# Other column orders for reads and sums of the first layer in one set of blocks

## The chip, the cores and the metric

The kernel runs on one core of a Trainium2 chip. The metric is the device time of one execution in microseconds (us). The engines are named as the profile names them: PE is TensorE (PEld its weight loads), DVE is VectorE, ACT is ScalarE, POOL is GpSimd, SP is SyncE, which here only issues DMAs.

## What is computed

Each of 8 batches of 2496 rows of 256 values is convolved with a filter by FFTs along the rows. The 19968 results then go through a mixture of experts: a gate picks two of eight experts for each row, and each expert is two matrix products with a ReLU between them.

```
X = np.fft.rfft(x, axis=1)
y = np.fft.irfft(X * F, n=x.shape[1], axis=1)
...
logits = x @ w_gate
noise_scale = np.log1p(np.exp(x @ w_noise))
noisy_logits = logits + noise_scale * noise
top2 = np.argpartition(-noisy_logits, 2, axis=1)[:, :2]
...
for e in range(E):
    for k in range(2):
        mask = top2[:, k] == e
        h = np.maximum(x[mask] @ w1[e], 0.0)
        out[mask] += top2_w[mask, k, None] * (h @ w2[e])
```

The sizes are D = 256, F = 1024 hidden values and E = 8 experts.

## The kernel before

The FFT of a batch is written as matrix products with small tables (`s1`, `kg0` to `kg2`, `t3`, `i2`), then come the gate and the routing of the batch (`gate`, `route`). They put the row numbers that each expert has to do into lists in DRAM. As soon as a batch is routed, the experts can work on blocks of 512 listed rows while the FFT of the next batches goes on beside them. `run` deals the blocks out in sets: set 1 has 2 blocks, set 2 another 10, set 3 another 4. Set 4, which starts when the fourth batch is routed, has 4 pairs, so 8 blocks; later sets follow up to the eighth batch, then the rests. Each block carries the number of its set in `ready`.

A block goes through `expert` like this. Its 512 rows are gathered from DRAM by GpSimd (line 1005), turned by a DMA transpose, and split into a rounded part `mxh` and a remainder `mxl` (lines 1066 and 1067), for each of the two halves `kc` of the 256 input values. Then the first layer runs over eight column blocks `f` of 128 hidden values. For each, `_mm3` is called for the two `kc`: six products (lines 123 to 125) with weights `w1h` or `w1l` as the standing operand and the 512 rows of `mxh` or `mxl` as the moving one. All six add into one bank `hps` of 128 x 512 fp32 sums. Two banks bear the tag `hps`; in these blocks every third sum uses the single bank `xps`, so three banks take turns. ACT writes the ReLU of the sums, rounded, into `hh` (line 1156), DVE the remainder into `hl` (line 1157). That eviction frees the bank.

The second layer takes 128 rows at a time: from set 4 on (`WIDE`), line 1183 multiplies `hh` with both parts of `w2` side by side, and line 1184 multiplies `hl` with the rounded part, for eight `f`. ACT and DVE add the two halves of the bank `yps` (lines 1188 and 1190), and GpSimd adds the rows into the output by an indirect DMA (line 1191).

The products of the FFT that the prediction speaks of: line 353 transposes 128 x 128 blocks next to one another into a bank; line 430 writes four results of 128 columns into a bank with `q3[:, :, 2 * j:2 * j + 2].rearrange("p b r -> p r b")`, so neighbours in time lie eight fp32 apart. In `route`, line 928 multiplies fp16 tables; in the first two batches the four tables `j` lie interleaved in a tile, so that both operands are read at a step of four fp16 values (8 bytes), in later batches they lie one behind another. Line 526 copies fp32 results as two 2-byte halves, read at a step of 4 bytes.

The order of each engine's instructions isn't written by hand here: the framework schedules them with a simulated timeline in which each engine works in order. The pace of FFT work against expert work is set by `PACE` and `FILL`. Waits are semaphores that the framework adds where tiles or banks are shared.

Of the kernel before, what the change touches and what calls it, by code (L numbers as in the profile page):

```python
# [15 lines left out]
AF = mybir.ActivationFunctionType  # L16
ALU = mybir.AluOpType
# [104 lines left out]
def _mm3(nc, o, lh, ll, rh, rl, start=True, stop=True):  # L122
    nc.tensor.matmul(o, lh, rh, start=start, stop=False)  # L123
    nc.tensor.matmul(o, lh, rl, start=False, stop=False)  # L124
    nc.tensor.matmul(o, ll, rh, start=False, stop=stop)  # L125


def f32v(ap):
    return ap.bitcast(F32)
# [9 lines left out]
BANKS = {"hps": 2, "yps": 2, "xps": 1, "fps": 3}  # L139

MOVES = {0: {"q3": "yps"}, 12: {"q3": "fps"}, 14: {"q3": "yps", "q4": "yps", "q5": "hps", "q6": "hps"}, 26: {"q4": "fps", "q5": "yps", "q6": "yps"}}


class Moe:
# [390 lines left out]
    def fft_stream(self):  # L535
# [105 lines left out]
        for t in range(max(plan) + 1):  # L641
            self.banks.update(MOVES.get(t, {}))
            for g in plan.get(t, []):
# [481 lines left out]
    def expert(self, parts, may, fill=None):  # L1125

        nc, P = self.nc, self.P
        self.parts, self.ahead, self.standing, self.early_l = parts, [], False, None
        self.fetch(lambda: True)
        cur = None  # L1130
        while self.ahead:
            if cur is None:
                cur = self.front(self.ahead[0], fill)
            ent = self.ahead.pop(0)
            blk, i = ent[:2]
            lt, n, nt, s, tabi, ready = blk
            w = 128 * nt
            w1, xT, w2st = cur
            if i == 0:
                w2, adds = [], []  # L1140
            ids, gate = lt[:, i], xT[2]
            if not self.ahead or self.ahead[0][3] or sum(len(a[2][0]) for a in self.ahead) < 4:
                self.fetch(may)
            third = ("xps", 1) if self.by_dma(ent) else ("yps", 2)
            hh = []
            for f in range(8):

                tag, bufs = ("hps", 2) if f % 3 < 2 else third
                p = self.PS.tile([128, 512], F32, name="hps", tag=tag, bufs=bufs)[:, :w]
                for kc in range(2):  # L1150
                    wh, wl = w1[f // 2]
                    o = (f % 2) * 128
                    _mm3(nc, p, wh[:, kc, o:o + 128], wl[:, kc, o:o + 128], *xT[kc], start=(kc == 0), stop=(kc == 1))
                h = P.tile([128, 512], R32, name="hh", bufs=8)[:, :w]
                l = P.tile([128, 512], R32, name="hl", bufs=8)[:, :w]
                nc.scalar.activation(h, p, AF.Relu)  # L1156
                v = nc.vector.scalar_tensor_tensor(l, p, 0.0, f32v(h), op0=ALU.max, op1=ALU.subtract)  # L1157
                if f == 4:
                    self.early_l = v
                hh.append((h, l))  # L1160
                if f % 2 and i == 0:
                    w2.append(self.wsplit(w2st[f // 2], "w2", f // 2))
                yield
            late = not self.ahead
            if late:
                self.fetch(lambda: True)
            if self.ahead:
                e2 = self.ahead[0]
                cur = (w1, self.turn(e2), None) if e2[1] else self.front(e2, fill if late else None)
            self.fetch(may)  # L1170
            yield
            for t in range(nt):


                wide = ready >= WIDE
                if wide or t % 2 == 0:
                    bank = self.PS.tile([128, 2, D], F32, name="yps", bufs=2)
                p = bank[:, 0 if wide else t % 2]
                for f in range(8):
                    h, l = (a[:, t * 128:(t + 1) * 128] for a in hh[f])  # L1180
                    hl = w2[f // 2][:, :, f % 2]
                    if wide:
                        nc.tensor.matmul(bank, h, hl, start=(f == 0), stop=False)  # L1183
                        nc.tensor.matmul(p, l, hl[:, 0], start=False, stop=(f == 7))  # L1184
                    else:
                        _mm3(nc, p, h, l, hl[:, 0], hl[:, 1], start=(f == 0), stop=(f == 7))
                o = self.slot("yo")
                nc.scalar.activation(o, p, AF.Copy, scale=gate[:, t])  # L1188
                if wide:
                    nc.vector.scalar_tensor_tensor(o, bank[:, 1], gate[:, t], o, op0=ALU.mult, op1=ALU.add)  # L1190
                a = nc.gpsimd.indirect_dma_start(  # L1191
                    out=self.io["out"][:BLK + ready * ROWS], out_offset=bass.IndirectOffsetOnAxis(ap=ids[:, t:t + 1], axis=0),
                    in_=o, in_offset=None, compute_op=ALU.add)
                for q in adds:
                    self.tc.declare_no_dep(a.ins, q.ins, reason="distinct rows of one expert")
                adds.append(a)
                self.lasta = a
                yield
# [109 lines left out]
```

## Time and profile before

| what | value |
|---|---|
| time, median of 3 runs | 2274.14 us (2271.94 to 2280.01) |
| span of the profiled execution, first to last instruction | 2263.0 us (the profile has no time of the whole execution beside it) |
| mean granted clock of TensorE | 0.992 |
| HBM read, written | 225.63 MB, 105.25 MB |
| products of the first layer in blocks of 512 rows (lines 123 to 125) | 1136 for each line |
| products of the second layer from set 4 on (lines 1183, 1184) | 2016 for each line |

How to read it: the page gives busy times of each engine over the span of one profiled execution. A row of a group shows line, engine, operation, output and inputs, shapes and count, then busy time in all and the mean of one in ns, then idle time of the engine just ahead of them and what ended it. A row of the timeline begins with its start and its length in us; products follow one another in a pipeline, so the length of one reaches into the next, and the distance of two starts is its pace. A row of stretches gives from:to, its length, and the busy time of PE, PEld, DVE, ACT and POOL with instruction counts, then the granted clock, the DMA share and GB/s. A row of waits names the engine and line that waited, the one that ended the wait, the sum in us, how often, and the longest. Rows of one source line give min/median/max in ns and the first and last start.

### The profile page before, as it was taken

How to read it: one execution, taken by the hardware profiler on the slowest of the kernel's cores; microseconds unless marked ns; L12 is line 12 of the kernel's file. 1: busy time of each engine (PE TensorE's matmuls, PEld its weight loads, DVE VectorE, ACT ScalarE, POOL GpSimd, SP SyncE). 2: the span in 40 equal slices, each digit the busy share in tenths (PEclk: the TensorE clock that was granted, in tenths of full speed). 3: DMA queues.
4: the chain of work that ended last, by engine and by line, in shares of the span. 5: the costliest groups of instructions: out<-in, count | busy, mean ns of one | idle time of the engine just before them, and what ended most of it. 6: DMA issues, size and time to landing. Idle time of an engine off the chain costs nothing.

```text
span 2263.0 us, 39152 instructions
## 1 busy us (share of the span) xinstructions
PE 2201.1 (97%) x12535; PEld 1838.5 (81%) x12535; DVE 1621.3 (72%) x3494; ACT 1239.4 (55%) x2425; POOL 953.5 (42%) x821
## 2 busy tenths in 40 slices
PE   8779999999999999999999999999999999999998
PEld 5438888888778788888888888888888888889997
DVE  4858689779777977697668866695555555667886
ACT  6765655666565455545544455443444444557876
POOL 4013344334233543344434544355454544554442
PEclk9989999999999999999999999999999999999999
DMA  8678778887686676668665667555555556768774
GB/s 242 189 229 203 186 185 190 205 201 169 144 223 156 151 170 154 149 142 178 143 146 121 134 131 165 108 125 121 124 117 115 116 127 125 180 158 244 217 212 130
DMA packets 436441, 368.99 MB, mean 163 GB/s; under 512 B 187675, under 2 KB 347395, under 8 KB 436227
## 3 DMA queue, kind: packets, MB, share of 16 engines
q1 hardware_dynamic: 374915, 282.01, 45.7%
q0 software_dynamic: 61312, 84.40, 23.2%
q8 instruction: 100, 1.64, 0.3%
q14 instruction: 114, 0.93, 0.1%
HBM read 225.63 MB, written 105.25 MB: 146 GB/s over the span
## 4 chain that ended last, share of the span: by engine, by line
PE 88%; ACT 3%; DMA 3%; DVE 3%; issue 2%; SPq 1%; POOL 0%; ACTq 0%; POOLq 0%; DVEq 0%
PE yps L1183 20%; PE hps L123 13%; PE hps L124 12%; PE hps L125 12%; PE yps L1184 10%; PE yps L123 2%; PE yps L125 2%; PE yps L124 2%; PE q L430 2%; PE q L494 1%; PE u L441 1%; DMA stage<-y,ids 1%; PE q L319 1%; PE q L518 1%; PE q L519 1%
## 5 line engine op out<-in xcount | busy, mean ns | idle before, releaser
L1191 POOL DMA_INDIRECT out<-stage,ids x316 | 535.8, 1696 | 450.8 <-DVE stage L1190 222.2
L1183 PE MATMUL yps<-w,hh 128*128 128x512 f32 x2016 | 710.7, 398 | 1.6 <-DVE stage L1190 1.4
L1005 POOL DMA_INDIRECT stage<-y,ids x316 | 337.2, 1067 | 538.4 <-DMA xt<-stage 403.7
L1184 PE MATMUL yps<-w,hl 128*128 128x256 f32 x2016 | 539.1, 282 | 0.0
L124 PE MATMUL hps<-mxl,w1h 128*128 128x512 f32 (+2 forms) x1424 | 530.5, 374 | 0.3 <-DVE mxl L1067 0.3
L125 PE MATMUL hps<-mxh,w1l 128*128 128x512 f32 (+2 forms) x1424 | 524.4, 370 | 0.0
L123 PE MATMUL hps<-mxh,w1h 128*128 128x512 f32 (+2 forms) x1424 | 518.8, 376 | 2.0 <-DVE hl L1157 1.6
L1157 DVE SCALAR_TENSOR_TENSOR hl<-hps,hh 128x512 fp32r<-128x512 f32 (+2 forms) x712 | 433.2, 624 | 94.2 <-ACT hh L1156 91.8
L1156 ACT ACTIVATE hh<-hps 128x512 fp32r<-128x512 f32 (+2 forms) x712 | 380.5, 553 | 205.1 <-PE hps L125 186.4
L1183 PEld LDWEIGHTS yps<-w,hh 128*128 128x128 f32 x2016 | 368.3, 188 | 80.4 <-issue 1.9
L1184 PEld LDWEIGHTS yps<-w,hl 128*128 128x128 f32 x2016 | 378.9, 189 | 28.6 <-issue 1.7
L1188 ACT ACTIVATE stage<-yps,gt 128x256 f32<-128x256 f32 x316 | 142.6, 478 | 368.1 <-PE yps L1184 213.6
L125 PEld LDWEIGHTS hps<-mxh,w1l 128*128 128x128 f32 x1424 | 268.2, 188 | 48.8 <-issue 0.6
L124 PEld LDWEIGHTS hps<-mxl,w1h 128*128 128x128 f32 x1424 | 268.7, 189 | 41.3 <-DVE mxl L1067 0.7
L123 PEld LDWEIGHTS hps<-mxh,w1h 128*128 128x128 f32 x1424 | 264.3, 189 | 45.5 <-DVE hl L1157 6.5
L1190 DVE SCALAR_TENSOR_TENSOR stage<-yps,gt,stage 128x256 f32<-128x256 f32 x252 | 115.9, 479 | 221.7 <-ACT stage L1188 220.6
L1113 ACT CAST w1h<-stage 128x512 fp32r<-128x512 f32 x188 | 116.6, 621 | 107.0 <-PE hps L124 57.1
L1114 DVE TENSOR_TENSOR w1l<-stage,w1h 128x512 fp32r<-128x512 f32 x188 | 128.0, 685 | 55.2 <-ACT w1h L1113 54.3
L1114 DVE TENSOR_TENSOR w<-stage,w 128x512 fp32r<-128x512 f32 x224 | 149.7, 684 | 9.9 <-ACT w L1113 9.7
L123 PE MATMUL yps<-w,hh 128*128 128x256 f32 x512 | 145.7, 288 | 3.2 <-ACT hh L1156 2.8
L1113 ACT CAST w<-stage 128x512 fp32r<-128x512 f32 x224 | 137.7, 637 | 9.8 <-DMA stage<-w 5.5
L124 PE MATMUL yps<-w,hh 128*128 128x256 f32 x512 | 142.9, 285 | 0.0
(226 smaller groups left out, 3004.9 us busy)
## 6 DMA issues: line engine op xcount, KB each, us to landing
stage<-w SPq DMA_DIRECT2D x412, 256.0 KB
x<-x SPq DMA_DIRECT2D x88, 256.0 KB
fd<-c SPq DMA_DIRECT2D x77, 240.0 KB
wb<-w SPq DMA_DIRECT2D x18, 1024.0 KB
fx<-fd SPq DMA_DIRECT2D x140, 128.0 KB
out<-z SPq DMA_DIRECT2D x24, 702.0 KB
y<-yt SPq DMA_DIRECT2D x40, 248.6 KB
y<-yt SPq DMA_DIRECT2D x40, 234.0 KB
```

The source lines that it names most:

```text
L123: nc.tensor.matmul(o, lh, rh, start=start, stop=False)
L124: nc.tensor.matmul(o, lh, rl, start=False, stop=False)
L125: nc.tensor.matmul(o, ll, rh, start=False, stop=stop)
L1005: self.pin(lambda: nc.gpsimd.indirect_dma_start(out=x.bitcast(I32), out_offset=None, in_=self.y[:BLK + ready * ROWS], in_offset=bass.Indir ...
L1113: nc.scalar.copy(h, sv)
L1114: nc.vector.tensor_sub(l, sv, f32v(h))
L1156: nc.scalar.activation(h, p, AF.Relu)
L1157: v = nc.vector.scalar_tensor_tensor(l, p, 0.0, f32v(h), op0=ALU.max, op1=ALU.subtract)
L1183: nc.tensor.matmul(bank, h, hl, start=(f == 0), stop=False)
L1184: nc.tensor.matmul(p, l, hl[:, 0], start=False, stop=(f == 7))
L1188: nc.scalar.activation(o, p, AF.Copy, scale=gate[:, t])
L1191: a = nc.gpsimd.indirect_dma_start(out=self.io["out"][:BLK + ready * ROWS], out_offset=bass.IndirectOffsetOnAxis(ap=ids[:, t:t + 1], axis= ...
```

## The change

Only blocks with `ready == 4` are touched, in `expert`. A table `WALKS` gives for each column block `f` an order in which the six products read their 512 moving rows (`read`) and one in which they write the sums (`put`). `walk` makes the operand's access pattern: "odd" takes every other row first and then the rest, a number i takes i rows of the first half, i of the second half, the next i of the first, and so on.

| f | moving rows are read | sums are written | pieces of the eviction |
|---|---|---|---|
| 0, 7 | in order | in order | 1 |
| 1 | every other one | in order | 2 |
| 2 | runs of 2, by turns from both halves | the same order, so each sum is at its own place | 1 |
| 3 | in order | runs of 2, by turns into both halves | 2 |
| 4, 5, 6 | runs of 2, 4, 8, by turns from both halves | in order | 2 |

Where `read` and `put` differ, the sums lie in another order in the bank than the rows have; `pairs` then cuts the eviction into two pieces of 256 columns, each with patterns on bank and tile that put the values back into order. Each piece is one ACTIVATE on ACT and one SCALAR_TENSOR_TENSOR on DVE.

```diff
+WALKED = 4
+WALKS = [(None, None), ("odd", None), (2, 2), (None, 2), (2, None), (4, None), (8, None), (None, None)]
+def walk(a, how):
+    if how is None:
+        return a
+    if how == "odd":
+        return a.rearrange("p (j two) -> p two j", two=2)
+    return a.rearrange("p (h j i) -> p j h i", h=2, i=how)
+def halves(a, how):
+    if how is None:
+        return [a[:, 256 * h:256 * h + 256] for h in range(2)]
+    a = a.rearrange("p (j h) -> p h j", h=2) if how == "odd" else a.rearrange("p (j h i) -> p h j i", h=2, i=how)
+    return [a[:, h] for h in range(2)]
+def pairs(p, h, l, read, put):
+    if read == put:
+        return [(p, h, l)]
+    sums, turned = (None, read) if read == "odd" else (read, None) if put is None else (None, put)
+    return list(zip(halves(p, sums), halves(h, turned), halves(l, turned)))
...
+                read, put = WALKS[f] if self.by_dma(ent) and ready == WALKED else (None, None)
...
-                    _mm3(nc, p, wh[:, kc, o:o + 128], wl[:, kc, o:o + 128], *xT[kc], start=(kc == 0), stop=(kc == 1))
+                    _mm3(nc, walk(p, put), wh[:, kc, o:o + 128], wl[:, kc, o:o + 128], *(walk(a, read) for a in xT[kc]),
+                         start=(kc == 0), stop=(kc == 1))
...
-                nc.scalar.activation(h, p, AF.Relu)
-                v = nc.vector.scalar_tensor_tensor(l, p, 0.0, f32v(h), op0=ALU.max, op1=ALU.subtract)
+                for pv, hv, lv in pairs(p, h, l, read, put):
+                    nc.scalar.activation(hv, pv, AF.Relu)
+                    v = nc.vector.scalar_tensor_tensor(lv, pv, 0.0, f32v(hv), op0=ALU.max, op1=ALU.subtract)
```

The new functions move the lines of the code: the eviction on ACT is line 1188 in the new kernel and on DVE line 1189, the second layer lines 1215 and 1216 with evictions in 1220 and 1222, and the FFT's lines lie 29 further down. The order of the instructions is the same up to the first block of set 4 and again after the last steps of the FFT; between these the scheduler places FFT work differently among the products.

The first place is ACT's queue in the first block of set 4, with the waits of each instruction. Before:

```order
L1156 ACTIVATE hh<-hps 128x512 [waits PE_49]
L323 CAST xh<-x 117x512 [waits DMAHW7_49,DVE_49,PE_49]
L362 COPY c_7090<-q_7086 120x512 [waits DMAHW6_49,PE_49,Activation_49]
L504 CAST th<-q_7107 120x512 [waits PE_49]
L1156 ACTIVATE hh<-hps 128x512 [waits PE_49] x2
L381 CAST th<-fx 128x512 [waits DMAHW2_49,DMAHW3_49,DVE_49,PE_49]
L526 COPY yt<-q_7148 117x4x256 [waits DMAHW0_49]
```

and in the changed kernel, where the sum of f = 1 comes in two pieces, that of f = 2 in one, and that of f = 3 in two whose tiles are written in runs of two:

```order
L1188 ACTIVATE hh<-hps 128x256 [waits PE_49]
L352 CAST xh<-x 117x512 [waits DMAHW7_49,DVE_49,PE_49]
L391 COPY c_7090<-q_7086 120x512 [waits DMAHW6_49,PE_49,Activation_49]
L1188 ACTIVATE hh<-hps 128x256 [waits DVE_49]
L533 CAST th<-q_7107 120x512 [waits PE_49]
L1188 ACTIVATE hh<-hps 128x512 [waits PE_49]
L1188 ACTIVATE hh<-hps 128x128x2 [waits PE_49]
L410 CAST th<-fx 128x512 [waits DMAHW2_49,DMAHW3_49,PE_49,Activation_49]
L555 COPY yt<-q_7148 117x4x256 [waits DMAHW0_49]
L1188 ACTIVATE hh<-hps 128x128x2 [waits DVE_49]
```

The second piece of a sum waits for DVE, which has to be done with the first piece, and other work of ACT stands between the two and behind them.

The second place is PE's queue a little later in that block: the second layer of the block (`yps`), which begins on its first sums, a product of the FFT with three parts, and the next sum (`hps`). Before:

```order
L1184 MATMUL yps<-w_9133,hl 128x256
L1183 MATMUL yps<-w_9133,hh 128x512
L1184 MATMUL yps<-w_9133,hl 128x256
L1183 MATMUL yps<-w_9133,hh 128x512 x2
L123 MATMUL hps<-mxh_8940,w1h 128x512
```

and in the changed kernel:

```order
L1216 MATMUL yps<-w_9135,hl 128x256
L1215 MATMUL yps<-w_9135,hh 128x512
L1216 MATMUL yps<-w_9135,hl 128x256
L422 MATMUL q_7205<-th,hl 128x512
L423 MATMUL q_7205<-tl,hl 128x512
L424 MATMUL q_7205<-th,hl 128x512
L1215 MATMUL yps<-w_9135,hh 128x512 x2
L123 MATMUL hps<-mxh_8940,w1h 128x512
```

The three products of the FFT step (lines 393 to 395 before) now stand ahead of the last two products of the second layer's piece and ahead of the sum; the same products are there in both orders.

## The prediction

> **What bounds the kernel now.** I read the page first: the busy time of each engine and the chain of work that ended last.
>
> ```profile
> span 2263.0 us, 39152 instructions
> PE 2201.1 (97%) x12535; PEld 1838.5 (81%) x12535; DVE 1621.3 (72%) x3494; ACT 1239.4 (55%) x2425; POOL 953.5 (42%) x821
> PE 88%; ACT 3%; DMA 3%; DVE 3%; issue 2%; SPq 1%; POOL 0%; ACTq 0%; POOLq 0%; DVEq 0%
> ```
>
> TensorE (PE) is busy 97% of the span and makes up 88% of the chain. So the question is whether PE gets more work or new waits in the stretch that the change touches. Its place comes from the evictions of the first layer (line 1157, one for each sum): 128 belong to the 16 blocks ahead of set 4, and set 4 has the 129th to the 192nd. Counted up to 650 and up to 890 us:
>
> ```profile
> L1157 DVE SCALAR_TENSOR_TENSOR hl<-hps,hh x128: 621/681/693, 169.1 to 649.2; 128x512 fp32r<-128x512 f32 x128
> L1157 DVE SCALAR_TENSOR_TENSOR hl<-hps,hh x192: 621/682/693, 169.1 to 881.1; 128x512 fp32r<-128x512 f32 x192
> ```
>
> So set 4 lies between 650 and 890 us. The second view is the busy time by stretches, the third the waits of PE from 640 us to the end.
>
> ```profile
> 640.00:890.00 250.00, 245.94 (x1361) 203.53 (x1360) 194.56 (x403) 138.51 (x261) 106.86 (x86) 1.00 0.72 168
> 735.00:775.00 40.00, 39.21 (x215) 31.61 (x214) 38.69 (x112) 16.02 (x31) 19.85 (x13) 1.00 0.64 144
> 890.00:1460.00 570.00, 569.21 (x3064) 470.07 (x3063) 420.01 (x873) 287.58 (x544) 248.43 (x203) 1.00 0.66 143
> 1460.00:2240.00 780.00, 779.75 (x4366) 670.20 (x4365) 518.92 (x1057) 421.74 (x879) 379.29 (x336) 1.00 0.65 154
> ...
> PE q L329 <- DVE xl L324: 1.6, 1, 1.6
> PE yps L1183 <- DVE stage L1190: 1.4, 3, 0.8
> PE q L327 <- ACT xh L323: 0.5, 1, 0.5
> PE q L494 <- ACT c L362: 0.5, 1, 0.5
> PE hps L123 <- DVE hl L1157: 0.5, 1, 0.5
> ```
>
> The columns are PE, PEld, VectorE (DVE), ScalarE (ACT) and POOL, then the granted clock, 1.00 throughout. In set 4 PE idles 4.1 us of 250, later 0.8 of 570 and 0.25 of 780. It waits once, 0.5 us, for the eviction that frees a bank of sums. DVE has 55 us free in set 4 and ACT 111; only from 735 to 775, where the routing of the next batch runs, is DVE full (38.7 of 40).
>
> **The products themselves.** Each block of set 4 makes eight sums of six products over 512 columns; with eight blocks that is 48 products for each column block f. The pace of one, and of what stands beside it, is read from the starts in the timeline of PE:
>
> ```profile
> 830.03 0.39 PE L123 MATMUL hps<-mxh,w1h 128*128 128x512 f32 x1
> 830.26 0.40 PE L124 MATMUL hps<-mxl,w1h 128*128 128x512 f32 x1
> 830.49 0.39 PE L125 MATMUL hps<-mxh,w1l 128*128 128x512 f32 x1
> ...
> 831.18 1.05 PE L430 MATMUL q<-cf,a 128*128 128x128 f32 x8
> 831.99 0.48 PE L1183 MATMUL yps<-w,hh 128*128 128x512 f32 x1
> 832.31 0.28 PE L1184 MATMUL yps<-w,hl 128*128 128x256 f32 x1
> ```
>
> Starts are 0.23 us apart: 0.45 ns a column (the 0.39 overlaps the next product). The change makes no product more; it can only alter this 0.23.
>
> Sums written in another order: f = 2 and 3, 96 products, in runs of two fp32 that hop between the two halves of a bank. The trace has a strided write already. Line 430 writes its 128 columns at a step of eight fp32, and line 353 writes as many side by side:
>
> ```profile
> 17.34 1.06 PE L353 MATMUL q<-ident,stage 128*128 128x128 f32 x8
> ```
>
> Eight rows take 1.05 us strided and 1.06 us side by side, so there the step costs nothing. But these are plain fp32 rows: 0.81 us / 8 = 0.10 us for 128 columns, 0.79 ns a column, slower than the 0.45 needed here. Bounds: nothing, if hopping writes keep up; (0.79 - 0.45) x 512 = 0.17 us a product if strided writes go no faster than line 430 shows, 96 x 0.17 = 17 us. A gain is excluded: the products keep their number of columns. I take nothing: line 430 leaves a new place at every element and loses nothing; here two neighbours come together, which at 0.45 ns makes one new place in 0.9 ns, fewer than it already bears.
>
> [...]
>
> Rows read in another order: f = 1 (every other row: a step of 8 bytes), f = 2 and 4 (runs of two), f = 5 and 6 (runs of four and eight): 5 x 48 = 240 products. No fp32 row of the trace reads its moving columns so. The nearest is line 928, fp16: in the first two batches both its operands are read at a step of 8 bytes, later side by side. One stretch of twelve of each, with the row behind it:
>
> ```profile
> 163.59 0.82 PE L928 MATMUL ra<-oc 117*128 117x56 f16 x12
> 164.24 0.66 PE L516 MATMUL q<-tf,cm 120*117 120x512 f32 x1
> ...
> 352.42 0.48 PE L928 MATMUL ra<-oc 117*128 117x56 f16 x12
> 352.74 0.46 PE L518 MATMUL q<-th,hl 120*117 120x512 f32 x1
> ```
>
> One takes 0.65 / 12 = 54 ns with the step and 0.32 / 12 = 27 ns without. Either its 128 weights or its 56 moving columns set the 54. If the weights do, the array reads at this step at 54 / 128 = 0.42 ns a column, still under the 0.45 needed, and the cost is nothing. If the moving columns do, it is 54 / 56 = 0.96 ns, and a product costs (0.96 - 0.45) x 512 = 0.26 us more: 144 products with steps or runs of 8 bytes (f = 1, 2, 4) make 37 us, all 240 make 62 us. I take nothing, the weights' reading: they are the longer operand, and their load rows alone are longer too (118 against 96 ns):
>
> ```profile
> L928 PEld LDWEIGHTS <-oc x44: 111/118/135, 163.6 to 179.9; 117*128 117x128 f16 x42, 39*128 39x128 f16 x2
> L928 PEld LDWEIGHTS <-oc x44: 93/96/101, 352.4 to 378.2; 117*128 117x128 f16 x42, 39*128 39x128 f16 x2
> ```
>
> [...]
>
> **The evictions in two pieces.** Where reading and writing orders differ (f = 1, 3, 4, 5, 6) a sum of 512 columns is evicted in two pieces of 256, on ACT and on DVE, 40 times.
>
> ```profile
> L1157 DVE SCALAR_TENSOR_TENSOR hl<-hps,hh 128x512 fp32r<-128x512 f32 x568 | 379.7, 683 | 83.6 <-ACT hh L1156 81.3 <-PE yps L125 1.4
> L1157 DVE SCALAR_TENSOR_TENSOR hl<-hps,hh 128x256 fp32r<-128x256 f32 x112 | 45.1, 418 | 7.1 <-ACT hh L1156 7.1
> L1156 ACT ACTIVATE hh<-hps 128x512 fp32r<-128x512 f32 x568 | 330.4, 601 | 186.4 <-PE hps L125 167.8 <-DVE stage L1053 10.0 <-DVE w L1114 3.0
> L1156 ACT ACTIVATE hh<-hps 128x256 fp32r<-128x256 f32 x112 | 42.1, 388 | 12.9 <-PE hps L125 12.9
> ```
>
> DVE: 2 x 418 - 683 = 153 ns more, x 40 = 6.1 us. ACT: 2 x 388 - 601 = 175 ns more, x 40 = 7.0 us. Both fit into the 55 and 111 us that the two have free in set 4, beside PE's products. If that cover were gone, 6.1 us of DVE would stand on the path. For steps inside a piece I add nothing: the copy of line 526 reads 2-byte elements at a step of 4 bytes in 1016 ns for 1024, and the 213 ns between the two ACT rows above, for 256 elements, give the same 0.8 ns an element.
>
> ```profile
> L526 ACT COPY yt<-q 117x1024 uint16<-117x1024 uint16 x80 | 81.3, 1016 | 32.7 <-PE q L520 25.6 <-PE q L516 5.6 <-PE q L494 0.7
> ```
>
> New is a wait: ACT's second piece waits for DVE's first (the order of ACT shows it). The hop from ACT to DVE is 0.04 us:
>
> ```profile
> 842.94 0.60 ACT L1156 ACTIVATE hh<-hps 128x512 fp32r<-128x512 f32 x1 [0.64 <-PE hps L125]
> 843.58 0.69 DVE L1157 SCALAR_TENSOR_TENSOR hl<-hps,hh 128x512 fp32r<-128x512 f32 x1 [1.31 <-ACT hh L1156]
> ```
>
> A sum was evicted in 0.60 + 0.04 + 0.68 = 1.33 us; now 0.39 + 0.42 + 0.39 + 0.42 + 3 x 0.04 = 1.73. Meanwhile ACT stands in order: behind the waiting piece are FFT copies, weight roundings and the second layer's evictions (line 1188), for which PE and POOL wait. Three banks take turns, so at the densest two other sums, 2 x 6 x 0.23 = 2.76 us, lie between a sum's end and the next use of its bank. 1.73 fits, with 1.0 us to spare. I charge only the full stretch: 11 sums are evicted there, 11 x 5/8 x 0.153 = 1.1 us on DVE, and I put all of it on the path.
>
> ```profile
> L1157 DVE SCALAR_TENSOR_TENSOR hl<-hps,hh x11: 677/680/691, 736.0 to 768.2; 128x512 fp32r<-128x512 f32 x11
> ```
>
> **The new order.** The longer evictions make the scheduler place FFT work and products anew from set 4 to the last FFT steps; no instruction is added by that, on SP's and POOL's queues neither. After plain fp32 rows the next fp32r product lasts longer: 831.99 to 832.31 is 0.32, not 0.23. Counted in the two orders, such changes go from 241 to 251: 10 x 0.09 = 0.9 us.
>
> **The sum.** 0 + 0 + 1.1 + 0.9 = +2.0 us on a span of 2263.0, so 2265. The profiled execution shows only its span; the median of the three runs, 2274.14, is 11.1 us above it, and with that distance kept the time is **2276 us**. A measurement of this kernel tells about 0.3% (6.8 us) from no change; +2 is inside.
>
> **The rivals.** (1) *Hopping writes are slow*: +17, 2293 us. For it: no row shows strided writes at 0.45 ns a column. Against it: line 430. [...] (2) *Reads at 8 bytes are slow*: +37, 2313 us. For it: the 54 ns of line 928. Against it: its longer weight loads. (3) *The chain of pieces stalls PE*, the slower case by one mechanism: if both DVE pieces of a sum stand behind one foreign instruction each (0.68, as line 1157 itself), the eviction takes 1.73 + 1.37 = 3.1 us and PE waits 0.34 at the next use of the bank; 40 x 0.34 = +14, 2290 us. It decides where more than 1.0 us of foreign work gets into the chain while sums come back to back. For it: DVE's full stretch. Against it: 0.5 us of such waiting before, and sums that on average come every 240 / 64 = 3.75 us. (4) *The new order is better*: from 640 us on PE idles only 4.1 + 0.8 + 0.25 us ahead of the tail, so all it can win is 5 us: 2271 us.
>
> **How the numbers follow.** Forecast 0.61; (1) 0.12; (2) 0.13; (3) 0.09; (4) 0.05, of which 0.03 by over 0.3%, together with what a tail might give. So faster 0.03, same 0.63, slower 0.34. The range runs from 2268, under (4), to 2300, over (1) with some of (3); it leaves out (2) and the faster end, 0.16.
>
> **What would show it.** In the profile after: starts of the products of f = 1 to 6 still 0.23 us apart; if (1) holds, those of f = 2 and 3 alone are slower, if (2) holds f = 1, 2 and 4. Pieces of 0.42 us on DVE and 0.39 on ACT. PE's wait for line 1189 of the new kernel under 2 us; tens of waits speak for (3). The stretch of set 4 as long as before within 3 us. I am wrong if PE's pace in that stretch changes at all.

## The result and the profile after

| | before | after |
|---|---|---|
| time, median | 2277.07 us, 4 runs (2271.94 to 2280.62) | 2295.08 us, 4 runs (2294.56 to 2299.34) |
| ratio | 1 | 1.0091, 95% interval 1.007 to 1.0111 |
| profiled execution, span | 2263.0 us | 2297.2 us (time of that execution 2299.34) |

The change makes the kernel 18 us slower by the medians and 21 by the ratio, 16 to 25 by its interval: 0.9%, well over the 0.3% of no change. That is inside the range of 2268 to 2300, but the likeliest case, no change that can be measured, did not come. The profile of before is of a quick execution (its span lies 14 us under the median), that of after is of the longest of its four, so the 34 us between the two spans overstate the change.

The first lines of the page of the changed kernel:

```profile
span 2297.2 us, 39267 instructions
PE 2230.0 (97%) x12535; PEld 1842.5 (80%) x12535; DVE 1624.9 (71%) x3534; ACT 1245.4 (54%) x2465; POOL 944.2 (41%) x821
```

PE does the same 12535 products and is busy 28.9 us longer, which has the same excess in it; DVE and ACT have their 40 instructions more and 3.6 and 6.0 us. The time of the stretch of set 4 by engine, as shown of before (PE, PEld, DVE, ACT, POOL, then the clock):

```profile
640.00:890.00 250.00, 245.66 (x1241) 187.42 (x1241) 184.72 (x417) 131.32 (x276) 94.66 (x78) 0.99 0.65 156
890.00:1460.00 570.00, 567.62 (x3072) 470.85 (x3072) 427.48 (x902) 292.12 (x553) 240.82 (x202) 1.00 0.63 144
```

PE is as busy in set 4 as before (245.66 against 245.94 us) and the clock is the same within 0.01, but it starts 1241 products there instead of 1361. It hardly waits more; products are slower. Which ones, the starts in the timeline of PE show, in the first block of set 4 (start, length, then what; f = 1, 2, 3, 4, 5 and 6 from top to bottom):

```profile
657.30 0.62 PE L123 MATMUL hps<-mxh,w1h 128*128 128x512 f32 x1
657.74 0.63 PE L124 MATMUL hps<-mxl,w1h 128*128 128x512 f32 x1
658.19 0.30 PE L123 MATMUL yps<-w,hh 128*128 128x256 f32 x1
...
669.14 0.51 PE L123 MATMUL hps<-mxh,w1h 128*128 128x512 f32 x1
669.48 0.50 PE L124 MATMUL hps<-mxl,w1h 128*128 128x512 f32 x1
...
672.77 0.39 PE L125 MATMUL hps<-mxh,w1l 128*128 128x512 f32 x1
673.00 0.39 PE L123 MATMUL hps<-mxh,w1h 128*128 128x512 f32 x1
...
676.57 0.50 PE L124 MATMUL hps<-mxl,w1h 128*128 128x512 f32 x1
676.90 0.51 PE L125 MATMUL hps<-mxh,w1l 128*128 128x512 f32 x1
...
679.72 0.41 PE L124 MATMUL hps<-mxl,w1h 128*128 128x512 f32 x1
679.97 0.41 PE L125 MATMUL hps<-mxh,w1l 128*128 128x512 f32 x1
...
682.57 0.41 PE L123 MATMUL hps<-mxh,w1h 128*128 128x512 f32 x1
682.81 0.41 PE L124 MATMUL hps<-mxl,w1h 128*128 128x512 f32 x1
```

From one start to the next it takes 0.44 us where every other row is read (f = 1), 0.34 and 0.33 with runs of two (f = 2, 4), 0.25 with runs of four (f = 5), 0.24 with runs of eight (f = 6), and 0.23 for f = 3, which only writes in another order. The medians over all such products of the trace, worked out from their starts and given in ns, are 232 in order, 452 for every other row, 332 for runs of two, 253 for four and 243 for eight. (The expectations below that have 0.445 us for every other row, 0.213 more than in order, take it from the two rows at the top.) With 48 products for each f that is 48 x (0.220 + 2 x 0.100 + 0.021 + 0.011) = **22 us** more PE time.

The last two views are the waits of PE from 640 us to the end, and the evictions in pieces:

```profile
PE hps L123 <- DVE hl L1189: 3.6, 12, 1.2
PE yps L1215 <- issue: 2.2, 9, 0.3
PE yps L123 <- ACT hh L1188: 2.2, 1, 2.2
PE yps L1215 <- DVE stage L1222: 1.4, 2, 1.2
PE yps L1215 <- ACT hh L1188: 1.0, 2, 0.7
```

```profile
L1189 DVE SCALAR_TENSOR_TENSOR hl<-hps,hh 128x256 fp32r<-128x256 f32 x192 | 78.0, 419 | 12.9 <-ACT hh L1188 12.3
L1188 ACT ACTIVATE hh<-hps 128x256 fp32r<-128x256 f32 x192 | 73.1, 396 | 37.9 <-PE hps L125 25.6 <-DVE hl L1189 11.2
```

These two rows also hold the 112 half-width evictions that the kernel had before; the 80 pieces alone take 421 ns on DVE and 402 on ACT, where half-width evictions took 418 and 388 before. The new wait of ACT for DVE is there, 11.2 us of it, but little of PE's hangs on the pieces. Of the 3.6 us for which PE waits for a bank, the first lies at 1003 us, and the last piece is evicted at 908. The 2.2 us for line 1188 end at 650 us, ahead of the first piece. Of the 1.0 us for which the second layer (line 1215) waits for line 1188, 0.7 is a wait for a second piece that stood behind other work of ACT (it ends at 740.65 us); the other 0.3 is for a sum evicted whole.

### The profile page after: what moved, and what is told of

It reads as the page before. It is cut to its first block, busy times and chain, and to the rows that moved or that the text cites. A ratio compares the mean times of both kernels' runs of the same rounds, so it can differ in the third digit from the quotient of the medians.

```text
span 2297.2 us, 39267 instructions
## 1 busy us (share of the span) xinstructions
PE 2230.0 (97%) x12535; PEld 1842.5 (80%) x12535; DVE 1624.9 (71%) x3534; ACT 1245.4 (54%) x2465; POOL 944.2 (41%) x821
## 4 chain that ended last, share of the span: by engine, by line
PE 67%; DVE 2%; issue 1%; DMA 0%; ACT 0%; POOL 0%; SPq 0%; POOLq 0%; another core or an unknown queue 0%; DVEq 0%; ACTq 0%
PE yps L1215 19%; PE hps L123 11%; PE hps L125 11%; PE hps L124 10%; PE yps L1216 10%; PE q L459 1%; PE q L523 1%; DVE hl L1189 0%; PE u L470 0%; PE q L547 0%; PE q L548 0%; PE q L549 0%; DVE w1l L1143 0%; PE q L422 0%; DVE oc L954 0%
## 5 line engine op out<-in xcount | busy, mean ns | idle before, releaser
L1034 POOL DMA_INDIRECT stage<-y,ids x316 | 328.6, 1040 | 574.0 <-DMA xt<-stage 411.4
L124 PE MATMUL hps<-mxl,w1h 128*128 128x512 f32 (+2 forms) x1424 | 539.5, 380 | 0.6 <-DVE mxl L1096 0.6
L125 PE MATMUL hps<-mxh,w1l 128*128 128x512 f32 (+2 forms) x1424 | 533.0, 376 | 0.0
L123 PE MATMUL hps<-mxh,w1h 128*128 128x512 f32 (+2 forms) x1424 | 527.3, 384 | 5.4 <-DVE hl L1189 4.8
L1188 ACT ACTIVATE hh<-hps 128x512 fp32r<-128x512 f32 (+2 forms) x752 | 387.7, 535 | 219.0 <-PE hps L125 187.6
L1189 DVE SCALAR_TENSOR_TENSOR hl<-hps,hh 128x512 fp32r<-128x512 f32 (+2 forms) x752 | 438.3, 599 | 93.4 <-ACT hh L1188 84.8
L1142 ACT CAST w1h<-stage 128x512 fp32r<-128x512 f32 x188 | 116.8, 622 | 103.4 <-PE hps L124 51.7
```

The source lines that it names most:

```text
L1034: self.pin(lambda: nc.gpsimd.indirect_dma_start(out=x.bitcast(I32), out_offset=None, in_=self.y[:BLK + ready * ROWS], in_offset=bass.Indir ...
L1142: nc.scalar.copy(h, sv)
L1188: nc.scalar.activation(hv, pv, AF.Relu)
L1189: v = nc.vector.scalar_tensor_tensor(lv, pv, 0.0, f32v(hv), op0=ALU.max, op1=ALU.subtract)
```

## The experiments

Which part makes the time, reads, writes, or pieces with the new order, was asked first; then what in a read makes it slow, and whether an order exists that is faster. `WALKS` stands for the table of the changed kernel, (read, put) for each f. Where medians of paces are given, they are worked out from the starts of all such products in the trace of that run. Runs e1 to e4 share a chip and 21 runs of the kernel before (2262.22 us), e5 to e7 share 7 (2262.24), e8 and e9 share 7 (2274.68).

### The pieces and the new order alone

```diff
+                cut, read, put = read != put, None, None
...
-                for pv, hv, lv in pairs(p, h, l, read, put):
+                for pv, hv, lv in zip(halves(p, None), halves(h, None), halves(l, None)) if cut else [(p, h, l)]:
```

Against the changed kernel: rows and sums in order everywhere, the same 40 evictions cut in two.

> All reads and sums of set 4 in order, but the sums of f = 1, 3, 4, 5 and 6 evicted in two plain halves of 256 columns, so the new instructions on ACT and DVE and the new order of the schedule are there without any pattern. Theory R (the moving reads are slow): within 4 us of the kernel before, all products of set 4 start 0.23 us apart. Theory E (the evictions in pieces and the new order cost the time): at least 10 of the 18 us, with PE waiting for evictions.

Measured: 2264.25 us (11 runs), ratio 1.0008, interval 0.9999 to 1.0017: +2 us, and at most 4. The waits of PE from 640 us on, of this kernel:

```profile
PE hps L124 <- DVE mxl L1096: 1.7, 1, 1.7
PE yps L1216 <- DVE stage L1223: 1.5, 3, 0.8
...
PE hps L123 <- DVE hl L1190: 0.4, 1, 0.4
```

The wait for the eviction (here line 1190) is 0.4 us, no more than before. So the pieces and the order that the scheduler makes of them are not the 18 us. This order is near that of the changed kernel but not the same: PE's queues differ from the 3831st product on. What the order of the changed kernel costs by itself is therefore known only as a difference, from the next run.

### The reads alone

```diff
+WALKS = [(None, None), ("odd", None), (2, None), (None, None), (2, None), (4, None), (8, None), (None, None)]
...
-                for pv, hv, lv in pairs(p, h, l, read, put):
+                for pv, hv, lv in [(p, h, l)]:
```

> The moving rows of f = 1, 2, 4, 5, 6 read as in the changed kernel, all sums written in order and evicted whole (the rows of a block stay mixed up, so the output differs). Theory R, from the paces in the changed kernel's trace (0.445 for every other row, 0.33 for runs of two, 0.253 and 0.243 for runs of four and eight, against 0.232): 48 x (0.213 + 2 x 0.10 + 0.021 + 0.011) = +21 us. Theory E: under +8 us, since neither pieces nor a new order are there.

Measured: 2283.98 us, ratio 1.0096 (1.0081 to 1.0112): +21.8 us. The order of the instructions is that of the kernel before, so set 4 can be laid beside it. Its evictions, counted up to the last of the 16 blocks ahead and up to the last of the set:

```profile
L1189 DVE SCALAR_TENSOR_TENSOR hl<-hps,hh x128: 627/683/704, 166.7 to 646.5; 128x512 fp32r<-128x512 f32 x128
L1189 DVE SCALAR_TENSOR_TENSOR hl<-hps,hh x192: 623/683/704, 166.7 to 898.5; 128x512 fp32r<-128x512 f32 x192
```

Set 4 takes 898.5 - 646.5 = 252.0 us; before it was 881.1 - 649.2 = 231.9. The 20 us are made in the set, and they stay to the end. Medians of the paces are 451 ns for every other row and 339, 254 and 243 for runs of two, four and eight. So the reads alone make as much as the whole change (18 to 21 us), in the order of before; for pieces, writes and the new order nothing is left that these runs can tell from zero.

### The writes alone

```diff
+WALKS = [(None, None), (None, 2), (None, "pair"), (None, 4), (None, 8), (None, 2), (None, "pair"), (None, None)]
...
+    if how == "pair":
+        return a.rearrange("p (j a i) -> p a j i", a=2, i=2)
...
```

Six of the eight f write their sums in runs of two, four or eight by turns into both halves, or in pairs at a step of 16 bytes.

> All moving rows read in order, sums written in runs of 2 by turns into both halves (f = 1, 5), runs of 2 at a step of four columns (f = 2, 6), runs of 4 and 8 by turns (f = 3, 4), evicted whole without putting the columns back (the output differs). Theory R and the trace of the changed kernel (f = 3 at 0.23 us): every product starts 0.23 us after the one ahead, time within 4 us of before. [...]

Measured: 2260.98 us, ratio 0.9998 (0.9989 to 1.0008), with 288 such products. The timeline of PE in one of these sums:

```profile
663.14 0.39 PE L123 MATMUL hps<-mxh,w1h 128*128 128x512 f32 x1
663.37 0.39 PE L124 MATMUL hps<-mxl,w1h 128*128 128x512 f32 x1
```

0.23 us apart; the median of every f is 232 or 233 ns. In this run writes in runs of two or more cost nothing; single columns were not tried.

### What in a read makes it slow

```diff
+WALKS = [(None, None), ("inline", None), ("pair", None), ("four", None), ("eight", None), (1, None), (2, None), (None, None)]
...
+    if how == "four":
+        return a.rearrange("p (j four) -> p four j", four=4)
+    if how == "eight":
+        return a.rearrange("p (j eight) -> p eight j", eight=8)
+    if how == "inline":
+        return a.rearrange("p (j i two) -> p j two i", i=2, two=2)
...
```

"inline" reads columns 0, 2, 1, 3, 4, 6, 5, 7 and so on; "pair" reads 0, 1, 4, 5, 8, 9, then the pairs left out; "four" and "eight" read every fourth and every eighth column; 1 reads single columns by turns from both halves.

> Only reads, each f another one: f = 1 columns 0,2,1,3 of each group of four (16 bytes), f = 2 runs of two at a step of 16 bytes, f = 3 and 4 every fourth and every eighth column (one column of each 16 bytes), f = 5 single columns by turns from both halves, f = 6 runs of two by turns from both halves; sums in order, evicted whole (the output differs). Theory W (each read fetches two neighbouring columns, a lone column costs a whole read): f = 1, 3, 4, 5 at 0.445 us a product, f = 2 and 6 as runs of two were, 0.33. [...] Theory H (the hop of 1 KB between the halves costs, not the small step): f = 2 at 0.23 and f = 6 at 0.33.

One run. The timeline of PE, first where "inline" (f = 1, to 662.72) passes into pairs (f = 2), then in f = 3, 4, 5 and 6:

```profile
662.49 0.39 PE L125 MATMUL hps<-mxh,w1l 128*128 128x512 f32 x1
662.72 0.62 PE L123 MATMUL hps<-mxh,w1h 128*128 128x512 f32 x1
663.15 0.63 PE L124 MATMUL hps<-mxl,w1h 128*128 128x512 f32 x1
663.61 0.63 PE L125 MATMUL hps<-mxh,w1l 128*128 128x512 f32 x1
...
668.38 0.66 PE L124 MATMUL hps<-mxl,w1h 128*128 128x512 f32 x1
668.84 0.66 PE L125 MATMUL hps<-mxh,w1l 128*128 128x512 f32 x1
...
672.06 0.61 PE L125 MATMUL hps<-mxh,w1l 128*128 128x512 f32 x1
672.49 0.61 PE L123 MATMUL hps<-mxh,w1h 128*128 128x512 f32 x1
...
675.96 0.38 PE L125 MATMUL hps<-mxh,w1l 128*128 128x512 f32 x1
676.17 0.38 PE L123 MATMUL hps<-mxh,w1h 128*128 128x512 f32 x1
...
678.28 0.50 PE L123 MATMUL hps<-mxh,w1h 128*128 128x512 f32 x1
678.61 0.50 PE L124 MATMUL hps<-mxl,w1h 128*128 128x512 f32 x1
```

The medians, in ns: "inline" 232, pairs at 16 bytes 451, every fourth 461, every eighth 432, runs of two by turns 332, and **single columns by turns 216**, less than the 232 in order. Both theories fall: W by the order 0, 2, 1, 3 at 232 and the single columns at 216, H by the pairs at 451. The time agrees with the paces: 48 x (0.219 + 0.229 + 0.200 + 0.100 - 0.016) = 35 us, and the run, 2295.98, stands 34 over before.

### How far apart the turns may be

```diff
+WALKS = [(None, None), (("hop", 4), None), (("hop", 8), None), (("hop", 16), None), (("hop", 64), None), (("parts", 4), None), (("hop", 256), None), (("hop", 128), None)]
...
+    if how[0] == "hop":
+        return a.rearrange("p (j h i) -> p j i h", h=2, i=how[1])
+    return a.rearrange("p (h j) -> p j h", h=how[1])
...
```

Single columns by turns from two places 16, 32, 64 or 256 bytes, 1 KB or 512 bytes apart, and for f = 5 from four places.

> Only reads, sums in order and evicted whole (the output differs). Single columns by turns from two places: f = 1 the places 16 bytes apart, f = 2 32 bytes, f = 3 64 bytes, f = 4 256 bytes, f = 7 512 bytes, f = 6 1 KB (in the run with lone columns 0.216 us); f = 5 by turns from four places 512 bytes apart. [...] Theory B (two reads at a time are only possible between places far enough apart): 0.44 for the near places, 0.216 from some distance on.

Measured, one run: 2260.86 us. The timeline of PE with two places 16 bytes apart (f = 1) and with four places (f = 5):

```profile
662.92 0.38 PE L123 MATMUL hps<-mxh,w1h 128*128 128x512 f32 x1
663.14 0.38 PE L124 MATMUL hps<-mxl,w1h 128*128 128x512 f32 x1
...
673.02 0.45 PE L123 MATMUL hps<-mxh,w1h 128*128 128x512 f32 x1
673.30 0.44 PE L124 MATMUL hps<-mxl,w1h 128*128 128x512 f32 x1
```

By the medians two places run at 216 ns at every one of the six distances, four places at 280. So at these six the distance plays no part, and B falls.

### What set the 54 ns of line 928

```diff
-                if bt < 2:
-                    ol, vv = (a.rearrange("p (l j) -> p l j", j=4) for a in (ol, vv))
-                else:
-                    ol, vv = (a.rearrange("p (j l) -> p l j", j=4) for a in (ol, vv))
+                by = "p (l j) -> p l j", "p (j l) -> p l j"
+                ol, vv = ol.rearrange(by[bt != 0], j=4), vv.rearrange(by[bt != 1], j=4)
...
```

The kernel before, where the first batch steps only the weights `ol` and the second only the moving `vv`. The line is 926 here.

> The kernel before, but of line 928's two operands only the weights lie interleaved (step of 8 bytes) in the first batch and only the moving columns in the second; the computation is the same. My reading (the weights set the 54 ns): 54 ns a product in the first batch, 27 in the second. The other reading (the moving columns set it): 27 in the first, 50 to 54 in the second, which 56 columns at the 0.87 ns that every other column takes in the changed kernel would give (49 ns).

Rows of the timeline of PE, in the first batch and in the second, each with the row behind it:

```profile
103.07 0.42 PE L926 MATMUL ra<-oc 117*128 117x56 f16 x8
103.33 1.14 PE L430 MATMUL q<-cf,ab 128*128 128x128 f32 x8
...
164.48 0.58 PE L926 MATMUL ra<-oc 117*128 117x56 f16 x8
164.89 0.66 PE L516 MATMUL q<-tf,cm 120*117 120x256 f32 x2
```

Stepped weights: 0.26 / 8 = 33 ns a product. Stepped moving columns: 0.41 / 8 = 51 ns (medians 33.5 and 52), against 55 with both and 26 with neither. The granted clock is 1.00 around the two rows of line 928 that the prediction shows; in this run the products of the first layer behind the row of the second batch start 0.23 us apart, as they do before in set 4 at a clock of 1.00:

```profile
166.72 0.40 PE L125 MATMUL hps<-mxh,w1l 128*128 128x512 f32 x1
166.95 0.39 PE L123 MATMUL hps<-mxh,w1h 128*128 128x512 f32 x1
```

The moving columns set the 54 ns. The time of this run, 2275.24, stands 13 us over before; its instructions come in another order from the first batch on, what makes the 13 us wasn't followed, and it isn't used.

### The faster order in the whole first layer

```diff
+def turns(a):
+    return a.rearrange("p (h j) -> p j h", h=2) if a.shape[1] == BLK else a
...
+                    _mm3(nc, p, wh[:, kc, o:o + 128], wl[:, kc, o:o + 128], *(turns(a) for a in xT[kc]), start=(kc == 0), stop=(kc == 1))
...
+                if w == BLK:
+                    hv, lv = (a.rearrange("p (h j) -> p h j", h=2) for a in (h, l))
+                    pv = p.rearrange("p (j h) -> p h j", h=2)
...
```

The kernel before with single columns by turns from both halves in every 512-row block; one eviction as before, which puts the values back.

> The kernel before with the moving rows of the first layer read one by one by turns from the two halves in all blocks of 512 rows; sums side by side, evicted whole with the bank read at a step of two columns, so the rows end up in order and the computation is the same. Theory P (PE's pace is what counts, and 0.216 holds everywhere): 3 x 1136 products x (0.232 - 0.216) = -54 us. Rival Q (with PE faster DVE and the evictions become the limit, or the stepped evictions are slower): under 20 us gained.

Measured: 2223.67 us (2216.71 to 2224.33, 4 runs), ratio 0.9831 (0.9814 to 0.9847): -38.6 us. The timeline of PE:

```profile
1005.42 0.38 PE L124 MATMUL hps<-mxl,w1h 128*128 128x512 f32 x1
1005.63 0.38 PE L125 MATMUL hps<-mxh,w1l 128*128 128x512 f32 x1
1005.85 0.38 PE L123 MATMUL hps<-mxh,w1h 128*128 128x512 f32 x1
```

0.215 us apart; over all 3408 products the median is 216 ns. 3408 x 0.016 gave the 54 us of P; 16 of them are missing in the medians of times. The profiled execution, 2216.71, shows 45.5 us. Its trace beside that of before has most of the rest: summed from each start to the next, without idle time, the 3408 products take 747.9 us instead of 799.6, so 51.7 less; but PE idles 3.8 us longer, and the products of the second layer take 3.6 more. Q falls. The median lies 7 us over the profiled execution; why stays open.

### The same in the second layer

```diff
-                    hl = w2[f // 2][:, :, f % 2]
+                    hl = w2[f // 2][:, :, f % 2].rearrange("p two (h j) -> p two j h", h=2)
...
+                o2, p2 = o.rearrange("p (h j) -> p h j", h=2), p.rearrange("p (j h) -> p h j", h=2)
...
```

Both layers by turns; the two evictions of the second layer put their values back.

> The kernel of the run before (first layer read by turns in all blocks of 512 rows), and besides that the weights of the second layer, there the moving operand, read by turns from two halves of 256 columns, 512 bytes apart; sums side by side, the evictions of the second layer read the bank at a step of two and put the columns in order (the computation is the same). Theory P: lines 1183 (0.232 to 0.216, 2016 times: -32 us) and 1184 (0.118 to 0.110, 2016 times: -16 us) gain too, so about -85 us against the kernel before the change. Rival Q: the weight loads (0.19 us each, one for each product) or the evictions hold PE, no more than -45 us.

Measured: 2189.8 us (2184.32 to 2193.35, 4 runs), ratio 0.9616 (0.9598 to 0.9635): **-84.9 us**, faster than both kernels. The page's busy times, the timeline of PE in the second layer, and one eviction group:

```profile
PE 2108.7 (96%) x12535; PEld 1828.2 (83%) x12535; DVE 1615.7 (74%) x3494; ACT 1234.4 (56%) x2425; POOL 970.6 (44%) x821
```

```profile
1805.54 0.38 PE L1191 MATMUL yps<-w,hh 128*128 128x512 f32 x1
1805.75 0.27 PE L1192 MATMUL yps<-w,hl 128*128 128x256 f32 x1
1805.86 0.38 PE L1191 MATMUL yps<-w,hh 128*128 128x512 f32 x1
```

```profile
L1165 DVE SCALAR_TENSOR_TENSOR hl<-hps,hh 128x512 fp32r<-128x512 f32 x568 | 380.3, 686 | 65.0 <-ACT hh L1164 61.9 <-issue 1.9 <-PE yps L125 0.5
```

PE is busy 92 us less than before (2108.7 against 2201.1). In the second layer a product over 512 columns takes 0.21 us and one over 256 takes 0.11 (medians 218 and 109 ns; in the kernel before 232 and 117). Q falls, though evictions begin to hold PE: it waits 8.2 us for line 1165, where before it waited 1.6 for line 1157. Reading a bank at a step of 8 bytes costs DVE and ACT nothing (686 ns against 683 and 601 against 601 in the first layer, 480 against 479 and 477 against 478 in the second).

### Is a slow read hidden anywhere

```diff
+WALKS = [("odd", None)] * 8
...
```

All eight f of set 4 read every other row, whole evictions.

> All eight column blocks of set 4 read every other row first, sums in order and evicted whole (the output differs). If the price is PE's alone and nothing hides it: 8 x 48 x 0.213 = +82 us. If part of it is hidden beside waits: less than 60.

Measured, one run: 2359.42 us, +84.7. With 8 x 48 = 384 products that is 0.22 us for each, what f = 1 lost in the trace of the changed kernel (452 against 232 ns); here the median is 452 too. Nothing in set 4 hides any of it, as far as one run shows.

## Why the prediction was right and where it was wrong

- **Reads in another order: this step failed.** "I take nothing, the weights' reading: they are the longer operand, and their load rows alone are longer too." The longer load rows were there (119 ns in the mean with only the weights stepped, 109 with only the moving columns), but they didn't set the pace: with only the weights stepped a product took 33 ns, with only the moving columns stepped 52 of the 54. A row in which two operands differ can't be put down to one of them, and the load rows overlap PE (busy 1838.5 and 2201.1 us of the same 2263.0). The other reading, rival (2), was the right mechanism at 22 us, not its 37: every other row costs 0.220 us a product (it said 0.26), runs of two 0.100 (0.26), runs of four and eight 0.021 and 0.011 (nothing). Its 0.96 ns a column of fp16 came near for fp32 only at the plain step (0.88). That a gain is excluded because "the products keep their number of columns" was said of the writes; for reads it would have been wrong (216 against 232 ns).
- **Writes in another order cost nothing: right**, by the writes alone (0.9998) and f = 3. Rival (1) is out. Line 430, with plain rows at 0.79 ns a column, pointed the right way at 0.45 too, for runs of two and more.
- **Pieces and new order, +2.0 us: right as a sum.** Pieces in an order near to that of the changed kernel make +2 (at most 4); the 1.1 and the 0.9 were not tested apart. The lengths of the pieces were 421 and 402 ns against 418 and 388, and the slack of the banks held: rival (3) is out, no PE wait for a bank `hps` lies between 640 and 1000 us. The wait for line 1189 came to 3.6 us, over the 2 that I had set, but later. Rival (4), at most 5 us to win, shows nowhere.
- **The sum** with the measured reads: 22 + 2 = 24 us, against 21 (16 to 25) by the ratio. The base held too: no cover, so every ns of a product's pace is on the path (21.8 for 22 by the paces in the reads alone, 84.7 for 0.22 x 384).
- **Chances.** Slower had 0.34, the rival that came 0.13. That the time lies in the range is luck: the range reached over rival (1), which did not happen, and the case that did lay outside at its own price of 2313. "I am wrong if PE's pace in that stretch changes at all" was the right test: it was met at once by the starts of f = 1.

Open: what in reading the moving columns sets these paces. In ns, in order and "inline" 232, by turns 216, four places 280, runs of two by turns 332 to 339, every other, fourth or eighth column and pairs at 16 bytes 432 to 461. None of W, H and B covers them all.

## What to carry to other kernels

In this kernel PE is busy 97% of the span and its products are fp32r (the type that the rows give for tiles such as `mxh` and `hl`), and the order of the moving columns belonged to the cost of a product: where it is like this, check the distance of two starts for any pattern that isn't plain. Steps and hopping pairs slowed a product to up to twice its time (332 to 461 ns against 232); single columns taken by turns from two places made it 7% faster (216 ns), and the eviction put the columns back without cost (686 against 683 ns on DVE, 601 against 601 on ACT). Of a row with two unusual operands, change one at a time before using its number.

## What the runs showed of the hardware

- Reading the moving columns by turns from two places is faster than in order: 216 against 232 ns for 512 columns of fp32r, at any of the six distances from 16 bytes to 1 KB; used in both layers it takes 3.8% off this kernel.
- The order 0, 2, 1, 3 costs nothing (232 ns), yet whole pairs with a gap of a pair cost as much as every other column (451 and 452 ns).
- Sums written in runs of two, four or eight that hop, or in pairs at a step of 16 bytes, cost nothing (232 ns, ratio 0.9998).
- Moving fp16 columns at a step of 8 bytes take 52 ns for 56 where plain ones take 26.
- ACT and DVE put columns back from a bank at a step of 8 bytes at no cost (601 against 601 and 686 against 683 ns for 512 columns, 477 against 478 and 480 against 479 for 256).
